# A sliding-window attention and gated-MLP kernel whose work is ordered by a list scheduler, with 64-key half-blocks in tiled arrays

## The chip, the core and the metric

The kernel runs on one core of a Trainium2 chip. The metric is the device time of one execution in microseconds; the kernel before took 304.65 us (median of 3 runs, 304.59 to 305.05). The engines are PE (TensorE, matrix products from SBUF into PSUM), PEld (its weight loads), DVE (VectorE), ACT (ScalarE), POOL (GpSimd) and SP (SyncE, which here only issues transfers). PSUM has eight banks of 128 partitions x 512 fp32 numbers. Each engine works through its own instruction stream in order.

## The reference

```python
def reference(A_x, A_wqkv, A_wo, B_x, B_w_gate, B_w_up, B_w_down):
    def _A_ref(x, wqkv, wo):
        B, S, D = x.shape
        H = 32; Dh = D // H; W = 256
        ...
        scores = jnp.einsum("bhqd,bhkd->bhqk", q, k) * (Dh ** -0.5)
        idx = jnp.arange(S)
        mask = (idx[:, None] - idx[None, :] >= 0) & (idx[:, None] - idx[None, :] < W)
        scores = jnp.where(mask[None, None], scores, -1e9)
        p = _softmax(scores, axis=-1)
        ...
    def _B_ref(x, w_gate, w_up, w_down):
        ...
        h = g * u
        ...
    x = A_x
    xn = _layernorm(x, axis=-1)
    return x + _A_ref(xn, A_wqkv, A_wo) + _B_ref(xn, B_w_gate, B_w_up, B_w_down)
```

There are 2048 tokens of width 512, 32 heads of 16 numbers, an inner width of 1792, all in bf16. A query sees itself and the 255 tokens before it. Attention and the gated product both read the normalised input, and both are added to x.

## The kernel before

Tokens go in four chunks T of 512, each of four blocks b of 128. All weights are loaded once and stay in SBUF (`setup`): the first blocks of x, then gate and up weights, the rest of x, down and output weights on SP's queue, Wqkv in three parts on ACT's queue (values first, then keys, then queries).

**Normalising.** `norm_stats` (L114, L115, DVE), `norm_scale` (L123, L125, POOL), `norm_apply` (L133, DVE) make xn. `norm_transpose` turns a block by four PE transposes (L145) into PSUM and copies it to xnT, on ACT for the first chunk (L148), on DVE later (L150).

**Projections.** `proj_v` (L157) gives values, which ACT copies (L159). `proj_qk` (L167) gives keys or queries for eight heads; DVE copies them and makes a second key tile Ko, in which the even heads are zeroed (L170, L171, L174). In the first chunk `proj_qk_block` (L183) does this block by block for the first eight heads alone, and their other 24 heads come later as fillers.

**Attention.** For a chunk, eight heads c, and even or odd heads par, there are three steps i. `scores` (L201) multiplies key blocks of 128 by the query blocks that see them, by the table GROUPS: a tuple is (key block, first and last query block, column). Four heads run side by side as row tiles of 32 partitions and write the four banks of S, the only score buffer. ACT takes the exponential of all four banks at once into P (L209, 2048 elements per partition), and POOL zeroes the triangles at the window's two edges by `affine_select` (L214, L218), 128 columns of four heads at a time. `values` (L234) multiplies the strips of three steps by V, four heads side by side as column tiles, and accumulates in one bank, `accb`. A column of ones in V gives the sums. DVE transposes the result in blocks of 32 (L245), divides (L247, L248) and transposes back to OT (L251).

**Gated product.** `gate` (L261), copied by DVE to gsb (L264), `up` (L270), multiplied by gsb into hT (L272), then `down` (L279) over hT, with the output projection `wo` (L284) added in the same bank; `store` adds x (L291) and sends the block out (L292). In the last chunk `finish_early` adds three quarters of the output projection and x (L303), and `finish_late` the last quarter. All dense results share three banks (`ps_m`).

**Order.** `run` does the first chunk's norm and projections block by block, then goes through 96 score steps. Between them it places dense work from the list `fillers` in proportion to the steps' weight, and `values` two steps after the last scores of a group. On the other engines the order is that in which the work was written.

## Time and profile before

| what | before |
|---|---|
| median of 3 runs | 304.65 us (304.59 to 305.05) |
| profiled execution: span from first to last instruction | 299.1 us |
| what lies around the span (median less span) | 5.55 us |
| PE busy | 274.7 us |
| DVE busy | 194.3 us |
| ACT busy | 181.5 us |
| POOL busy | 156.8 us |
| ACT's exponentials (L209) | 96, 170.0 us |
| POOL's selects (L214, L218) | 240, 154.6 us |

The profile lists one execution. A group is a source line with its engine, its tiles and shape; "x4" counts instructions, and the bracket at the end of a timeline row is the idle time of the engine just before it and what ended it. Matmuls are pipelined: the duration of one contains its way through the array, so durations in a row overlap, and the distance between starts says what one costs.

### The profile page before, as it was taken

How to read it: one execution, taken by the hardware profiler on the slowest of the kernel's cores; microseconds unless marked ns; L12 is line 12 of the kernel's file. 1: busy time of each engine (PE TensorE's matmuls, PEld its weight loads, DVE VectorE, ACT ScalarE, POOL GpSimd, SP SyncE). 2: the span in 40 equal slices, each digit the busy share in tenths (PEclk: the TensorE clock that was granted, in tenths of full speed). 3: DMA queues.
4: the chain of work that ended last, by engine and by line, in shares of the span. 5: the costliest groups of instructions: out<-in, count | busy, mean ns of one | idle time of the engine just before them, and what ended most of it. 6: DMA issues, size and time to landing. Idle time of an engine off the chain costs nothing.

```text
span 299.1 us, 5877 instructions
## 1 busy us (share of the span) xinstructions
PE 274.7 (92%) x2424; PEld 119.6 (40%) x2460; DVE 194.3 (65%) x362; ACT 181.5 (61%) x118; POOL 156.8 (52%) x266
## 2 busy tenths in 40 slices
PE   6569989999999999999999999999999999999992
PEld 5333333433433444444344444443444443344440
DVE  3238898985823599984942489985763357877325
ACT  1247566568766756669566666758766675756610
POOL 3115565455565556656555466655556555555620
PEclk9999999999999999999999999999999999999998
DMA  7999000000000100000000000000000000000001
GB/s 234 370 369 324 3 3 0 3 0 2 1 20 18 37 0 2 1 2 2 0 19 19 20 18 3 0 2 1 2 0 20 35 20 1 2 0 2 2 0 70
DMA packets 10506, 12.17 MB, mean 41 GB/s; under 512 B 496, under 2 KB 10480, under 8 KB 10480
## 3 DMA queue, kind: packets, MB, share of 16 engines
q1 hardware_dynamic: 8896, 10.23, 10.1%
q10 hardware_dynamic: 1584, 1.57, 1.7%
q8 instruction: 19, 0.31, 0.4%
q14 instruction: 7, 0.06, 0.1%
HBM read 9.70 MB, written 2.10 MB: 39 GB/s over the span
## 4 chain that ended last, share of the span: by engine, by line
PE 68%; ACT 17%; DVE 6%; DMA 3%; issue 3%; POOL 1%; ACTq 1%; DVEq 0%
ACT P L209 16%; PE psd L279 15%; PE up L270 12%; PE gp L261 11%; PE S L201 10%; PE accb L234 7%; PE qkp L167 6%; DMA Wqkv<-in_A_wqkv_dram 3%; PE vp L157 2%; PE psd L284 2%; DVE at L245 1%; PE xTp L145 1%; DVE hT L272 1%; DVE st L114 1%; PE qkb L183 1%
## 5 line engine op out<-in xcount | busy, mean ns | idle before, releaser
L209 ACT ACTIVATE P<-S 128x2048 bf16<-128x2048 f32 (+2 forms) x96 | 170.0, 1771 | 86.8 <-PE S L201 79.1
L214 POOL TENSOR_SCALAR_AFFINE_SELECT P<-P 128x512 bf16<-128x512 bf16 x128 | 81.8, 639 | 75.2 <-ACT P L209 74.6
L218 POOL TENSOR_SCALAR_AFFINE_SELECT P<-P 128x512 bf16<-128x512 bf16 x112 | 72.8, 650 | 42.4 <-ACT P L209 42.4
L261 PE MATMUL gp<-xnT,Wg 128*128 128x512 bf16 x213 | 57.1, 380 | 1.4 <-DVE gsb L264 0.5
L270 PE MATMUL up<-xnT,Wu 128*128 128x512 bf16 x216 | 57.3, 380 | 0.5
L279 PE MATMUL psd<-Wd,hT 128*128 128x512 bf16 x213 | 51.7, 380 | 1.4 <-issue 1.3
L272 DVE TENSOR_TENSOR hT<-up,gsb 128x512 bf16<-128x512 f32 x56 | 38.5, 687 | 11.0 <-PE up L270 8.0
L245 DVE STREAM_TRANSPOSE at<-accb 128x512 f32<-128x512 f32 x32 | 22.9, 715 | 32.6 <-PE accb L234 32.2
L264 DVE CAST gsb<-gp 128x512 bf16<-128x512 f32 x56 | 38.1, 680 | 3.7 <-PE gp L261 3.4
L270 PEld LDWEIGHTS <-Wu 128*128 128x128 bf16 x224 | 19.9, 98 | 25.8 <-issue 5.4
L279 PEld LDWEIGHTS <-hT 128*128 128x128 bf16 x224 | 19.8, 97 | 25.9 <-issue 5.3
L261 PEld LDWEIGHTS <-Wg 128*128 128x128 bf16 x224 | 19.8, 98 | 25.0 <-issue 6.0
L167 PE MATMUL qkp<-xnT,Wqkv 128*128 128x512 bf16 x117 | 27.5, 380 | 0.5 <-issue 0.5
L234 PE MATMUL accb<-P,V 128*17 128x384 bf16 (+2 forms) x704 | 25.4, 276 | 0.0
L291 DVE TENSOR_TENSOR y<-psd,x 128x512 bf16<-128x512 f32 x12 | 8.3, 692 | 23.2 <-PE psd L284 23.2
L201 PE MATMUL S<-Q,Ko 32*128 32x256 bf16 (+2 forms) x352 | 18.4, 275 | 3.8 <-ACT P L209 3.6
L201 PE MATMUL S<-Q,K 16*128 16x256 bf16 (+2 forms) x352 | 18.4, 275 | 2.6 <-ACT P L209 2.4
L234 PEld LDWEIGHTS <-V 128*17 128x17 bf16 x704 | 13.8, 90 | 8.7 <-issue 5.5
L167 PEld LDWEIGHTS <-Wqkv 128*128 128x128 bf16 x120 | 10.7, 98 | 13.7 <-issue 2.5
L157 PE MATMUL vp<-Wqkv,xnT 128*128 128x512 bf16 x61 | 15.9, 392 | 0.3 <-issue 0.2
L201 PEld LDWEIGHTS <-Ko 32*128 32x128 bf16 x352 | 6.9, 92 | 22.6 <-issue 22.1
L201 PEld LDWEIGHTS <-K 16*128 16x128 bf16 x352 | 6.6, 92 | 22.6 <-issue 22.5
(44 smaller groups left out, 172.2 us busy)
## 6 DMA issues: line engine op xcount, KB each, us to landing
out_dram<-y SPq DMA_DIRECT2D x16, 128.0 KB, 1.7
Wg<-in_B_w_gate_dram SPq DMA_DIRECT2D x2, 896.0 KB, 9.9
Wu<-in_B_w_up_dram SPq DMA_DIRECT2D x2, 896.0 KB, 11.5
Wd<-in_B_w_down_dram SPq DMA_DIRECT2D x1, 1792.0 KB, 17.7
Wqkv<-in_A_wqkv_dram ACTq DMA_DIRECT2D x3, 512.0 KB, 6.0
x<-in_A_x_dram SPq DMA_DIRECT2D x1, 1024.0 KB, 14.6
x<-in_A_x_dram SPq DMA_DIRECT2D x4, 128.0 KB, 5.1
x<-in_A_x_dram SPq DMA_DIRECT2D x1, 512.0 KB, 8.2
```

Of the source, the lines that this page charges most:

```text
L167: nc.tensor.matmul(ps[:], lhsT=self.Wqkv[:, k, lo:lo + 128], rhs=self.xnT[T][:, k, :], start=(k == 0), stop=(k == 3))
L201: nc.tensor.matmul(S[:, e, col:col + n], lhsT=(self.Ko if par else self.K)[U][rows, c, 128 * j:128 * j + 128], rhs=self.Q[T][rows, c, 128 ...
L209: nc.scalar.activation(out=P[:, :, lo:hi], in_=S[:, :, lo:hi], func=ACT.Exp, scale=0.25)
L214: nc.gpsimd.affine_select(out=P[:, :, j:j + 128], in_=P[:, :, j:j + 128], pattern=[[0, 4], [1, 128]], compare_op=ALU.is_ge, fill=0.0, base ...
L218: nc.gpsimd.affine_select(out=P[:, :, j:j + 128], in_=P[:, :, j:j + 128], pattern=[[0, 4], [-1, 128]], compare_op=ALU.is_gt, fill=0.0, bas ...
L234: nc.tensor.matmul(acc[32 * e:32 * e + 17, 128 * q0:128 * q0 + n], lhsT=self.V[U][:, v, 8 * c + 2 * e + par, 0:17], rhs=P[:, e, col:col + ...
L245: nc.vector.transpose(out=at.rearrange("p b r -> p (b r)"), in_=acc[:])
L261: nc.tensor.matmul(ps[:], lhsT=self.Wg[:, k, 128 * f:128 * f + 128], rhs=self.xnT[T][:, k, :], start=(k == 0), stop=(k == 3))
L264: nc.vector.tensor_copy(out=self.gsb[:], in_=ps[:])
L270: nc.tensor.matmul(ps[:], lhsT=self.Wu[:, k, 128 * f:128 * f + 128], rhs=self.xnT[T][:, k, :], start=(k == 0), stop=(k == 3))
L272: nc.vector.tensor_tensor(out=self.hT[T][:, f, :], in0=ps[:], in1=self.gsb[:], op=ALU.mult)
L279: nc.tensor.matmul(self.psd[:], lhsT=self.hT[T][:, f, 128 * b:128 * b + 128], rhs=self.Wd[:, f, :], start=(f == 0), stop=False)
```

## The change

The whole program is written anew around a list scheduler that runs while the program is built. Each piece of work on DVE, ACT, POOL and SP is an `Op` with what it depends on and, for each engine that could do it, a duration from a table in the file; PE's work is a list of `Dense` pieces, of `Sums` (the down and output projections), score batches and value steps. `loop` always takes the piece that can start first by these figures and writes it to the engine's stream. The order that results is fixed; on the chip the engines wait for one another by semaphores as before.

- **Half-blocks.** A key block has 64 keys, and `layout` says which query blocks of 64 it meets: (key block, first query block, how many, column). A score matmul holds the 64 keys of an even and an odd head in one stationary tile of 32 rows x 128 columns; keys are stored twice, each with the other head's rows zeroed (`i_keys`, written straight from PSUM by ACT or DVE). There are 76 score batches instead of 96, five for a chunk and eight heads (four in the first chunk).
- **Value steps.** One step takes both heads: eight tiles of 64 rows x 32 columns, into two banks. There are 16 value steps with 96 matmuls each (72 in the first chunk) instead of 32 with 24 (16). There is no bank of its own for them: four banks are shared by dense results and values.
- **V in column halves.** `add_v` projects 64 tokens for even and 64 for odd heads side by side, 16 matmuls of 256 columns for a block instead of four of 512.
- **Masks.** A batch with four masked blocks gets two ANDs on DVE with mask tiles (56 in all, 512 elements per partition); the others get POOL selects on 64 partitions (240 of 256 elements and 8 of 512).
- **Transposes.** The first chunk is turned by PE as before, the other three by 12 transposing DMAs on SP's queue.
- **First chunk.** Keys and queries of all 32 heads are projected block by block, 128 matmuls of 128 columns. Scores begin after that. The root of the variance is taken by ACT and DVE instead of POOL, with one more table load on ACT. Wqkv is loaded in parts on both queues between the blocks of x.
- **Copies** from PSUM go to DVE or ACT as the scheduler finds; 15 of the 56 gate copies go to ACT. P has seven buffers instead of five.
- **End.** The last value step is followed by 83 dense matmuls; the last block is summed in two column parts (320 and 192) and stored by two queues.

```diff
-GROUPS = (
-    ((-2, 0, 0, 0), (0, 0, 2, 128)),
-    ((-1, 0, 1, 0), (2, 2, 3, 256)),
-    ((1, 1, 3, 0), (3, 3, 3, 384)),
-)
+MM = 0.2158
+SWITCH = 0.11
+PE_LAT = {"V": 0.22, "A": 0.31}
+LAT = 0.06
+KEYS_COPY = {"V": (0.68, 0.76), "A": (0.63, 0.70)}
+PSUM_COPY = {"V": (0.605, 0.69), "A": (0.49, 0.60)}
...
+def layout(T):
+
+
+    if T == 0:
+        return [[(2, 2, 4, 0), (4, 4, 4, 4)], [(0, 0, 5, 0), (5, 5, 3, 5)],
+                [(1, 1, 5, 0), (6, 6, 2, 5), (7, 7, 1, 7)], [(3, 3, 5, 0), (2, 6, 1, 5)]]
+    return [[(3, 3, 5, 0), (-3, 0, 2, 5), (-4, 0, 1, 7)], [(2, 2, 5, 0), (6, 6, 2, 5), (7, 7, 1, 7)],
+            [(0, 0, 5, 0), (5, 5, 3, 5)], [(1, 1, 5, 0), (-2, 0, 3, 5)], [(-1, 0, 4, 0), (4, 4, 4, 4)]]
...
+def masked(batch):
+
+
+    return sorted((at + i, (q + i - k) // 4) for k, q, m, at in batch for i in range(m) if q + i - k in (0, 4))
...
+    PBUFS = 7
+    WINDOW = 4
+    PACE = 2.9
+    SHARE = 1.0
+    FEED = 0.1
+    HOLD = 0.2
+    TURN = 0.2
...
+        self.S = psum.tile([128, 4, 512], F32, name="S")
+        self.M = [psum.tile([128, 512], F32, name=f"M{i}") for i in range(4)] + [self.S[:, 3, :]]
...
+        load(nc.sync, self.x[0:64, 0, :], xv[0:64, 0, :])
+        load(nc.scalar, self.x[64:128, 0, :], xv[64:128, 0, :])
+        load(nc.sync, self.x[:, 1, :], xv[:, 1, :])
+        qkv(nc.sync, 1024, 0, 2)
+        qkv(nc.scalar, 1024, 2, 4)
+        qkv(nc.scalar, 512, 2, 4)
+        qkv(nc.sync, 512, 0, 2)
+        load(nc.sync, self.x[:, 2, :], xv[:, 2, :])
+        qkv(nc.sync, 0, 0, 4)
+        load(nc.sync, self.x[:, 3, :], xv[:, 3, :])
...
+    def i_scores(self, T, c, batch):
+
+        for k, q, m, at in batch:
+            U, j = divmod(8 * T + k, 8)
+            for e in range(4):
+                rows = slice(32 * e, 32 * e + 32)
+                self.nc.tensor.matmul(
+                    self.S[:, e, 64 * at:64 * (at + m)],
+                    lhsT=self.K[U % 3][rows, c, j].rearrange("p l t -> p (l t)"),
+                    rhs=self.Q[T % 2][rows, c, 64 * q:64 * (q + m)],
+                    start=True, stop=True, tile_position=(32 * e, 0), skip_group_check=True)
...
+    def i_select(self, P, lane, kind, at, n):
+        v = P[64 * lane:64 * lane + 64].rearrange("p e (b q) -> p e b q", q=64)[:, :, at:at + 4 * n - 3:4, :]
+        sign = -1 if kind else 1
+        self.nc.gpsimd.affine_select(out=v, in_=v, pattern=[[0, 4], [0, n], [sign, 64]], base=0, fill=0.0,
+                                     compare_op=ALU.is_gt if kind else ALU.is_ge, channel_multiplier=-sign)
+
+    def i_and(self, P, at, step, n, row):
+        v = P.bitcast(I16).rearrange("p e (b q) -> p e b q", q=64)[:, :, at:at + (n - 1) * step + 1:step, :]
+        m = self.masks[:, row:row + n, :].unsqueeze(1).to_broadcast([128, 4, n, 64])
+        self.nc.vector.tensor_tensor(out=v, in0=v, in1=m, op=ALU.bitwise_and)
...
+    def i_values(self, T, c, strips, banks):
+        rest = sorted(((P, s) for P, batch in strips for s in batch), key=lambda x: x[1][2])
...
+        for n, (P, (k, q, m, at)) in enumerate(segments):
+            U, j = divmod(8 * T + k, 8)
+            for lane in range(2):
+                rows = slice(64 * lane, 64 * lane + 64)
+                for e in range(4):
+                    self.nc.tensor.matmul(
+                        banks[lane][32 * e:32 * e + 17, 64 * q:64 * (q + m)],
+                        lhsT=self.V[U % 3][rows, j, 4 * c + e, 0:17],
+                        rhs=P[rows, e, 64 * at:64 * (at + m)],
+                        start=n == 0, stop=n == len(segments) - 1, tile_position=(64 * lane, 32 * e),
+                        skip_group_check=True)
...
+    def i_keys(self, e, T, c, lane, in_, blocks=slice(0, 8)):
+
+        own = self.own[:, lane:lane + 1]
+        out = self.K[T % 3][:, c, blocks, lane, :]
+        in_ = in_.rearrange("p c (j t) -> p c j t", t=64)
+        if e == "A":
+            self.nc.scalar.activation(out=out, in_=in_, func=ACT.Copy, scale=own)
+        else:
+            self.nc.vector.tensor_scalar(out=out, in0=in_, scalar1=own, scalar2=None, op0=ALU.mult)
...
+    def loop(self):
+        while True:
+            best, now0 = None, self.first_s is None
+            for o in self.waiting:
+                t = self.when(o.deps)
+                if t is None:
+                    continue
+                for e, (took, lat) in o.on.items():
+                    at = max(t, self.free[e])
+                    key = (at + (0.3 if e == "A" and len(o.on) > 1 and not now0 else 0.0) + (self.HOLD if o.rank and now0 else 0.0), o.rank, t)
+                    if best is None or key < best[0]:
+                        best = (key, o, e, at)
...
+            if best is None:
+                break
+            _, o, e, at = best
+            took, lat = o.on[e]
+            o.start, o.eng, o.end = at, e, at + lat + LAT
+            self.free[e] = at + took
+            self.waiting.remove(o)
+            self.log.append((at, e, took, o.name))
+            if self.live:
+                o.emit(e)
...
+    def do_scores(self, at):
+        g = self.g
...
+        hi = 64 * max(s[3] + s[2] for s in batch)
+        took = 0.000833 * 4 * hi
+        ex = self.op(f"exp{g}", {"A": (took + 0.06, took + 0.18)}, [o], lambda e: self.nc.scalar.activation(
+            out=P[:, :, 0:hi], in_=self.S[:, :, 0:hi], func=ACT.Exp, scale=0.25), rank=0)
+        self.at_["S", g] = ex
+        last = ex
+        if len(masked(batch)) > 3:
+            for m in ands(batch):
+                cost = 4 * 64 * m[2] * 0.00055 + 0.07
+                last = self.op(f"and{g}", {"V": (cost, cost + 0.08)}, [ex, last, ("masks",)], lambda e, m=m: self.i_and(P, *m), rank=1)
...
+    def do_values(self, at):
+        v, banks = self.v, [self.take_bank(), self.take_bank()]
+        self.v += 1
+        T, c = self.pairs[v]
...
+        ts = []
+        for par in range(2):
+            t = self.op(f"tr{v}", {"V": (0.63, 0.71)}, [o] + ts, lambda e, par=par: nc.vector.transpose(
+                out=self.at[:, :, par, :], in_=self.M[banks[par]].rearrange("p (b r) -> p b r", r=32)), rank=1)
+            self.frees(t, banks[par])
...
+            def project(i, lo, tok=tok):
+                for k in range(4):
+                    for c in range(4):
+                        self.nc.tensor.matmul(
+                            self.M[i][:, 128 * c:128 * c + 128], lhsT=self.Wqkv[:, k, lo + 128 * c:lo + 128 * c + 128],
+                            rhs=self.xnT[0][:, k, tok], start=k + c == 0, stop=k == 3, skip_group_check=True)
...
+    def norms(self, T):
+        w = T % 2
+        begin = [("gate", T - 1, 0)]
+        st = [self.op(f"st{T}.{b}", {"V": (0.96, 1.05)}, begin, lambda e, b=b: self.i_stats(4 * T + b, self.mv[w]),
+                      rank=8) for b in range(4)]
+        r = self.op(f"rs{T}", {"G": (1.05, 1.1)}, st, lambda e: self.i_root(w, 4 * T, 4), rank=0)
+        for b in range(4):
+            ap = self.op(f"ap{T}.{b}", {"V": (0.38, 0.48)}, [r], lambda e, b=b: self.i_apply(4 * T + b), rank=7)
+            deps = [ap] + ([("up", T - 2, NF - 1)] if T > 1 else [])
+            self.at_["xnT", T, b] = self.op(f"dt{T}.{b}", {"S": (1.5, 3.0)}, deps, lambda e, b=b: (
+                self.nc.sync.dma_start_transpose(out=self.xnT[w][:, :, 128 * b:128 * b + 128], in_=self.xn[b][:])),
+                rank=1)
+
...
+    def add_v(self, T, b, land=0.0):
+
+        def emit(i):
+            for k in range(4):
+                for jj in range(2):
+                    tok = slice(128 * b + 64 * jj, 128 * b + 64 * jj + 64)
+                    w = self.Wqkv[:, k, 1024:1536].rearrange("p (h l d) -> p l h d", l=2, d=16)
+                    for lane in range(2):
+                        self.nc.tensor.matmul(self.M[i][64 * lane:64 * lane + 64, 256 * jj:256 * jj + 256],
+                                              lhsT=self.xnT[T % 2][:, k, tok], rhs=w[:, lane], start=k + jj == 0,
+                                              stop=k + jj == 4, tile_position=(0, 64 * lane), skip_group_check=True)
```

**PE around a boundary inside a value step.** Before, in a value step of a later chunk (accb is its one bank, P the strips, V1 and V2 the values of two chunks), a stretch of four matmuls passes to the next key block:

```order
L234 LDWEIGHTS V1_913
L234 MATMUL accb_116<-P_2340,V1_913 17x128
L234 LDWEIGHTS V2_1872
L234 MATMUL accb_116<-P_2340,V2_1872 17x384
L234 LDWEIGHTS V2_1872
```

In the new program, inside a value step, the same weights' block passes from the even heads' bank M0 to the odd heads' bank M2:

```order
L253 MATMUL M0_111<-P3_90,V1_79 17x256
L253 LDWEIGHTS V1_79
L253 MATMUL M0_111<-P3_90,V1_79 17x256
L253 LDWEIGHTS V1_79
L253 MATMUL M2_113<-P3_90,V1_79 17x256
```

Four tiles with one bank became eight tiles with two, and the matmuls of a stretch are those of one 64-key block.

**ACT around the third chunk's projections.** Before, it copies V alone (vp is the bank of values, S the scores):

```order
L209 ACTIVATE P<-S 128x4x256
L209 ACTIVATE P<-S 128x2048 x22
L159 ACTIVATE V_1872<-vp 128x32x16 x2
L209 ACTIVATE P<-S 128x2048
L159 ACTIVATE V_1872<-vp 128x32x16 x2
L209 ACTIVATE P<-S 128x2048 x23
```

In the new program it takes copies of all kinds between exponentials (M are the four shared banks, gsb the gate's copy):

```order
L290 ACTIVATE K_77<-M_112,own 128x8x64
L506 ACTIVATE P_92<-S 128x2048
L209 ACTIVATE V_80<-M_113 128x32x16
L506 ACTIVATE P_93<-S 128x2048
L506 ACTIVATE P_87<-S 128x2048
L209 ACTIVATE Q_73<-M_114 128x512
L506 ACTIVATE P_88<-S 128x2048
L209 ACTIVATE Q_73<-M_113 128x512
L506 ACTIVATE P_89<-S 128x2048
```

One copy at most stands between two exponentials there; K, Q and gsb came over from DVE.

**SP.** Before, the loads are followed by the stores alone:

```order
L68 DMA Wu<-in_B_w_up_dram 128x4x896
L69 DMA x<-in_A_x_dram 128x8x512
L70 DMA Wd<-in_B_w_down_dram 128x14x512
L71 DMA Wo<-in_A_wo_dram 128x4x512
L292 DMA out_dram<-y 128x512 x16
```

In the new program the transposing DMAs of the three later chunks stand between loads and stores:

```order
L685 DMA_TRANSPOSE xnT0_81<-xn3_97 128x4x128
L800 DMA out_0_dram<-y_1505 128x512
L800 DMA out_0_dram<-y_1664 128x512
L800 DMA out_0_dram<-y_1704 128x512
L800 DMA out_0_dram<-y_1868 128x512
L685 DMA_TRANSPOSE xnT1_82<-xn0_94 128x4x128
L800 DMA out_0_dram<-y_2548 128x512
L685 DMA_TRANSPOSE xnT1_82<-xn1_95 128x4x128
```

Each transposing DMA waits for its normalised block, and what follows on SP waits behind it.

850 lines of the change are left out of this document (511 added, 339 removed).

## The prediction

> **What bounds the kernel now.** I read the busy row first, then TensorE's order of time in one steady stretch, then the waits, and last the two ends of the span.
>
> ```profile
> span 299.1 us, 5877 instructions
> PE 274.7 (92%) x2424; PEld 119.6 (40%) x2460; DVE 194.3 (65%) x362; ACT 181.5 (61%) x118; POOL 156.8 (52%) x266
> PEclk9999999999999999999999999999999999999998
> PE 68%; ACT 17%; DVE 6%; DMA 3%; issue 3%; POOL 1%; ACTq 1%; DVEq 0%
> ```
>
> TensorE is busy for 92% at full clock, and it holds 68% of the chain that ended last. No other engine passes 65%. But matmuls overlap, so what each stretch really costs is the distance from its start to the next start, on the steady timeline of PE (start, duration, instruction, idle before it):
>
> ```profile
> 116.88 1.03 PE L270 MATMUL up<-xnT,Wu 128*128 128x512 bf16 x4
> 117.84 0.40 PE L201 MATMUL S<-Q,K 16*128 16x384 bf16 x8
> 118.22 1.02 PE L261 MATMUL gp<-xnT,Wg 128*128 128x512 bf16 x4
> 119.08 1.03 PE L270 MATMUL up<-xnT,Wu 128*128 128x512 bf16 x4
> 120.30 0.40 PE L201 MATMUL S<-Q,Ko 32*128 32x128 bf16 x8 [0.19 <-ACT P L209]
> 120.63 1.04 PE L261 MATMUL gp<-xnT,Wg 128*128 128x512 bf16 x4
> 121.50 1.03 PE L270 MATMUL up<-xnT,Wu 128*128 128x512 bf16 x4
> 122.37 0.39 PE L145 MATMUL xTp<-ident,xn 128*128 128x128 bf16 x4
> 122.75 0.40 PE L201 MATMUL S<-Q,Ko 32*128 32x256 bf16 x8
> 123.08 0.83 PE L234 MATMUL accb<-P,V 128*17 128x128 bf16 x24
> 123.85 0.39 PE L261 MATMUL gp<-xnT,Wg 128*128 128x512 bf16 x1
> ```
>
> The price of one dense matmul of 512 columns comes from an unbroken run in the chain of waits:
>
> ```profile
> 283.95 3.02 PE psd L279 x14
> ```
>
> That is 3.02/14 = 0.216 us, so a column costs 0.216/512 = 0.42 ns. In the steady rows four dense matmuls take 0.87 us, and 0.96 us ahead of scores (116.88 to 117.84): entering the tiled mode costs 0.10. A score step of 512 columns takes 0.33 us (120.30 to 120.63); 0.21 is columns, 0.12 leaving. So a score step between dense work costs 0.43. The 24 value matmuls (four side by side, 1536 columns, 0.64 us) take 0.77, again 0.13 over the columns. Four transposes take 0.38 in this place.
>
> The only repeated wait on PE is that of scores for the exponential that empties S, their one buffer (total, times, longest):
>
> ```profile
> ACT P L209 <- PE S L201: 79.1, 82, 1.9
> PE S L201 <- ACT P L209: 6.1, 23, 0.6
> ```
>
> This view counts from the modelled end of a matmul. At 120.30 it shows 0.19, while the starts lie 1.22 apart instead of 0.96, so 0.26 is lost. With 0.07 more for each of 23, I take 8 us. The cycle behind it:
>
> ```profile
> 118.37 1.88 ACT L209 ACTIVATE P<-S 128x2048 bf16<-128x2048 f32 x1 [1.92 <-PE S L201]
> ```
>
> From the start of the scores (117.84) to the exponential 0.53, then 1.88, then 0.05 to the next scores: 2.46 us between two score steps at least.
>
> **The change part by part.** *Dense work* stays: gate, up, down and output projection and the later q and k are the same 832 matmuls' worth of 512 columns; nothing is gained. The first chunk's q and k become 128 matmuls of 128 columns; the row for eight of those is below (0.44 us, 0.055 each), so 7.0 us against 24 x 0.216 + 32 x 0.055 = 6.9. Zero.
>
> *Attention columns.* Before: 80 score steps at 0.43 and 16 shorter ones of the first chunk (384 or 256 columns, so 0.38 or 0.33), 40.0 us; 24 value steps at 0.77 and 8 of the first chunk:
>
> ```profile
> 30.07 0.67 PE L234 MATMUL accb<-P,V 128*17 128x384 bf16 x16
> 30.67 0.39 PE L270 MATMUL up<-xnT,Wu 128*128 128x512 bf16 x1
> ```
>
> at 0.60, 23.3 us. Together 63.3. With 64-key blocks a query block meets five half-blocks (320 keys) instead of three blocks (384): 2560 columns for a head group instead of 3072, and 76 score steps instead of 96. The 16 value steps run eight tiles at once, 2560 columns or 1920. By columns: 72 x 0.43 + 4 x 0.38 = 32.5; 12 x (1.07 + 0.13) + 4 x (0.80 + 0.12) = 18.1; together 50.6, a gain of 12.7.
>
> But a stretch of 64 columns lasts 27 ns, and weights for it must be loaded meanwhile. What a weight load takes, and how loads and matmuls begin in the first 0.03 us of a value step (two windows of the same step):
>
> ```profile
> L234 PEld LDWEIGHTS <-V x704: 87/92/92, 30.1 to 290.2; 128*17 128x17 bf16 x176
> 114.38 0.23 PE L234 MATMUL accb<-P,V 128*17 128x128 bf16 x4
> 114.37 0.11 PEld L234 LDWEIGHTS <-V 128*17 128x17 bf16 x8 [0.21 <-issue]
> ```
>
> In the window to 114.39 four matmuls have started, and by 114.40 eight loads: tiles start together, but only one set is loaded ahead. So I let no stretch pass in under 0.09 us. Of the 12 stretches of a value step (5, 2, 1, 5, 2, 1, 5, 3, 5, 3, 4, 4 blocks) six are shorter: +0.22 each step, +0.17 in the first chunk, +0.04 for each of 28 score batches with three stretches; 4.4 us. **Term: -8.3** (from -12.7 to +11, the upper end in the rivals).
>
> *Transposes on PE*: 48 of 64 go to DMAs. Twelve times four, between 4 x 0.055 = 0.22 and 0.38: **-3.2** (-2.6 to -4.6). Their copies from PSUM leave DVE. The transposing DMA has no row here; the nearest is a plain one of the same 128 KB:
>
> ```profile
> out_dram<-y SPq DMA_DIRECT2D x16, 128.0 KB, 1.7
> ```
>
> In the new order some 35 us of PE work lie between the first gate matmul and the first use of the next chunk's transposed input. Statistics and scaling take 9 to 14 of it, so about 25 are left for four transposes: hidden at 1.7 us each, late from 6 us each. They stand on SP ahead of output stores, and only those queue behind them.
>
> *Score waits.* In the new order of PE, pricing what lies between two score steps with the rows above gives 2.59 us (ten dense matmuls) at the least and mostly 3.02 (twelve), all over 2.46. ACT's 76 exponentials fit, and a copy of 0.6 fits the 0.53 in which scores are computed. Late here and there: 1.5 us stay. **Term: -6.5** (-8 to 0).
>
> *The start.* PE before the first scores:
>
> ```profile
> 10.37 0.61 PE L183 MATMUL qkb<-xnT,Wqkv 128*128 128x128 bf16 x4 [1.65 <-DMA Wqkv<-in_A_wqkv_dram]
> 13.97 0.61 PE L183 MATMUL qkb<-xnT,Wqkv 128*128 128x128 bf16 x8 [0.69 <-ACT xnT L148]
> 14.41 1.03 PE L157 MATMUL vp<-Wqkv,xnT 128*128 128x512 bf16 x4
> 16.27 0.40 PE L145 MATMUL xTp<-ident,xn 128*128 128x128 bf16 x4 [0.84 <-DVE xn L133]
> 17.36 0.61 PE L183 MATMUL qkb<-xnT,Wqkv 128*128 128x128 bf16 x8 [0.68 <-ACT xnT L148]
> 21.40 0.34 PE L201 MATMUL S<-Q,K 16*128 16x384 bf16 x4
> ```
>
> From 10.37 to 21.40, 11.0 us, the work is 28 x 0.055 + 16 x 0.216 + 12 x 0.055 = 5.7; 5.3 are waits for the norm chain. Now PE holds 2.6 us of q, k, v work per block (32 x 0.055 + 4 x 0.216) while the next is normalised, and it need not wait for the last third of Wqkv before the values. First scores come when all four blocks are projected, about 17 us, but with 5.2 us of what used to follow already done and eight gate matmuls. **Term: -7** (0 to -9).
>
> *Values of V in column halves*: 256 matmuls of 256 columns in pairs, the same columns, 8 more mode changes: **+1**. If their 256 weight loads, about 0.09 like those above, stood one by one, a pair would take 0.18 for 0.11: +9.
>
> *Masks.* POOL's 240 selects become 248 at half width:
>
> ```profile
> L214 POOL TENSOR_SCALAR_AFFINE_SELECT P<-P 128x512 bf16<-128x512 bf16 x128 | 81.8, 639 | 75.2 <-ACT P L209 74.6
> L78 POOL TENSOR_SCALAR_AFFINE_SELECT ident<-ident 128x128 bf16<-128x128 bf16 x1 | 0.3, 292 | 0.1
> ```
>
> Between 0.29 and 0.64, so 0.41 for 256: some 102 us, hidden. DVE gains 56 ANDs and two masked copies for K, loses 15 gate copies to ACT and the separate Ko:
>
> ```profile
> L264 DVE CAST gsb<-gp 128x512 bf16<-128x512 f32 x56 | 38.1, 680 | 3.7 <-PE gp L261 3.4
> L171 DVE TENSOR_SCALAR Ko<-K,odd x15: 353/354/825, 23.5 to 218.9; 128x512 bf16<-128x512 bf16 x15
> ```
>
> An AND costs 0.35 to 0.83 (the row's least and most; I take 0.53): +30. Thirteen V copies and seven more for K at 0.68: +14; 15 gate and 9 Q copies to ACT -16, Ko -8, transposed copies -5. DVE rises to about 210 us of a shorter span: over 75%, still behind PE. But dense results and value results now share four banks, and a value step keeps two until DVE has transposed them: **+1.5** (0 to +12).
>
> *The end.*
>
> ```profile
> 292.87 0.95 PE L284 MATMUL last<-Wo,OT 128*128 128x512 bf16 x3 [0.70 <-DVE OT L251]
> 294.04 0.38 PE L284 MATMUL last<-Wo,OT 128*128 128x512 bf16 x1 [0.22 <-DVE y L291]
> 295.83 0.69 DVE L291 TENSOR_TENSOR y<-last,y 128x512 bf16<-128x512 f32 x1 [0.66 <-DMA out_dram<-y]
> ```
>
> PE waits 0.92, the last add waits 0.66 for a buffer and handles 512 columns; now 83 matmuls cover the last transposes, and the last tile goes out in two parts: **-2.5** (0 to -3).
>
> Sum: -8.3 - 3.2 - 6.5 - 7 + 1 + 1.5 - 2.5 = -25.0. The profiled execution has a span of 299.1; the median is 304.65, so 5.55 lie outside the span and stay. 304.65 - 25.0 = 279.65: **280 us**. Its own range: 272 if weight loads and banks cost nothing; 288 if the start gains nothing.
>
> **The rivals.** *A: value matmuls pass one by one.* 24 matmuls in 0.64 us is 27 ns each, so the average of the old kernel can't exclude it. 96 x 0.027 = 2.56 instead of 1.29 in twelve steps, 72 x 0.027 = 1.92 instead of 0.97 in four: +19, **299 us**. The four that started within 0.01 us speak against it. By the Trainium skill, "TensorE: Matmul & The Clock Gate", "Wait — 56ns, not 53.3ns?", matmuls never start under about 25 ns apart however few columns they have; by that estimate the time would be about 297. The four starts in 0.01 us disagree with it for tiles. Chance 0.07.
>
> *B: DVE holds the banks.* If each of 16 value steps finds one more operation of 0.6 us ahead of its transposes, PE stands 16 x 0.6 = 10 us: **290 us**. For: DVE over 75%, ANDs up to 0.83. Against: the copies moved to ACT. Chance 0.13.
>
> *C: slower, by the transposing DMAs.* If a transpose takes t, the second chunk's first projections wait 4t - 25 us on PE. The gain of 25 is gone at t = 12.5; at 14 it is 31, **311 us**. For: no row shows one. Against: 1.7 us for the plain store, seven times less. Chance 0.05. The Trainium skill, "VectorE: DVE Perf Modes", "The three transpose paths", gives 1309 ns for a 128x128 crossbar transpose; four for an instruction and four instructions would be an estimated 21 us, inside the 25. No run so far shows one.
>
> *D: the new order doesn't hold on the chip*, since its queues are fixed and waits return elsewhere: start, score waits and end gain nothing, and banks cost 10.5: -8.3 - 3.2 + 1 + 10.5 = 0, **304.65 us**, no change. Chance 0.02.
>
> **How the numbers follow.** The forecast has 0.73. A measurement can tell about 0.2% (0.6 us). Faster holds the forecast, A and B: 0.93; same 0.02 (D); slower 0.05 (C). The range, 270 to 295, runs from the lower bounds of start and banks through B; A, C and D lie outside, 0.14, and the forecast's own tails.
>
> **What would show it.** Right: score steps between dense work still at about 0.43, value steps 1.3 to 1.5 us, hardly a wait of scores for the exponential, first scores near 17 us, transposes landing in a few us. Wrong: value steps over 2 us (A); dense matmuls that wait for DVE (B); a gap ahead of the second chunk's projections (C); exponentials further apart than 3 us (D).

## The result, and the profile after

| | before | after |
|---|---|---|
| median | 304.73 us (304.59 to 305.05) | 266.35 us (266.16 to 267.99) |
| profiled execution: span | 299.1 us | 264.0 us (266.31 with what lies around it) |

The ratio is 0.878 (95% interval 0.872 to 0.884): 38.4 us less. The forecast was 280 us, and its range ended at 270. The direction and most of the mechanisms were right; the gain was half as large again as forecast, and which terms were too small is the subject of what follows.

The page of the new kernel, with its busy row, the granted clock and the chain that ended last:

```profile
span 264.0 us, 7965 instructions
...
PE 256.2 (97%) x3420; PEld 131.7 (50%) x3456; DVE 189.2 (72%) x366; ACT 166.4 (63%) x124; POOL 119.3 (45%) x272
...
PEclk9999999999999999999999999999999999999999
...
PE 93%; DMA 2%; issue 2%; ACT 1%; DVE 1%; SPq 0%; DVEq 0%; ACTq 0%
```

TensorE went from 92% to 97% busy and from 68% to 93% of the chain; ACT's 17% of the chain fell to 1%. All waits of PE by the view of waits (total, times, longest):

```profile
PE M L215 <- issue: 1.7, 11, 0.2
PE M L205 <- PEq L827: 0.8, 1, 0.8
PE M L632 <- DVE xn L281: 0.6, 1, 0.6
```

The row of scores waiting for the exponential (6.1 us, 23 times) has no successor, and no dense matmul waits for DVE to empty a bank. The 1.7 us of "issue" stand where the record of a first dense matmul is missing. The steady timeline of PE, in the same place as the forecast's:

```profile
125.04 1.90 PE L215 MATMUL M<-xnT,Wqkv 128*128 128x512 bf16 x8
126.77 1.03 PE L215 MATMUL M<-xnT,Wg 128*128 128x512 bf16 x4
127.73 0.40 PE L223 MATMUL S<-Q,K 32*128 32x320 bf16 x12
128.06 1.29 PE L253 MATMUL M<-P,V 64*17 64x256 bf16 x96
129.28 1.04 PE L215 MATMUL M<-xnT,Wu 128*128 128x512 bf16 x3
```

Start to start: eight dense matmuls 1.73 (0.216 each, as before), four ahead of scores 0.96, scores 0.33, and the whole value step 1.22 (1.22 and 1.23 where no record is missing). A value step of the first chunk takes 0.94:

```profile
32.99 1.01 PE L253 MATMUL M<-P,V 64*17 64x256 bf16 x72
33.93 1.04 PE L215 MATMUL M<-xnT,Wg 128*128 128x512 bf16 x3
```

The start of PE, and its end with DVE's last add and the last store:

```profile
8.12 2.84 PE L647 MATMUL M<-xnT,Wqkv 128*128 128x128 bf16 x48
10.80 0.39 PE L632 MATMUL M<-ident,xn 128*128 128x128 bf16 x4
11.03 1.95 PE L647 MATMUL M<-xnT,Wqkv 128*128 128x128 bf16 x32
...
17.54 0.40 PE L223 MATMUL S<-Q,K 32*128 32x256 bf16 x8
```

```profile
257.56 3.08 PE L215 MATMUL M<-Wo,OT 128*128 128x512 bf16 x15
...
260.48 0.49 PE L215 MATMUL S<-Wo,OT 128*128 128x192 bf16 x4
261.14 0.35 DVE L793 TENSOR_TENSOR xn<-S,x 128x192 bf16<-128x192 f32 x1
261.52 0.37 ACTq L800 DMA_DIRECT2D out_dram<-xn  x1
```

First scores come at 17.54 instead of 21.40, with the q and k of every head already projected, but the V of one block only instead of four. After the last matmul's end (260.97) 3.0 us are left; before it was 294.42 and 4.7. Last, the groups of masks on the two engines, from the page, and the transposing DMAs from the view of DMA issues (count, median us to landing):

```profile
L232 POOL TENSOR_SCALAR_AFFINE_SELECT P<-P 64x256 bf16<-64x256 bf16 (+1 forms) x248 | 112.3, 455 | 106.6 <-ACT P L506 94.3
...
L238 DVE TENSOR_TENSOR P<-P,masks 128x512 int16<-128x512 int16 x56 | 22.3, 406 | 8.6 <-ACT P L506 8.6
```

```profile
xnT<-xn SPq DMA_TRANSPOSE x12, 3.5
```

### The profile page after: what moved, and what is told of

Same layout as the page of the kernel before. It is cut to its first block, busy times and chain, and to the rows that moved or that the text cites. A ratio compares the mean times of both kernels' runs of the same rounds, so it can differ in the third digit from the quotient of the medians.

```text
span 264.0 us, 7965 instructions
## 1 busy us (share of the span) xinstructions
PE 256.2 (97%) x3420; PEld 131.7 (50%) x3456; DVE 189.2 (72%) x366; ACT 166.4 (63%) x124; POOL 119.3 (45%) x272
## 4 chain that ended last, share of the span: by engine, by line
PE 93%; DMA 2%; issue 2%; ACT 1%; DVE 1%; SPq 0%; DVEq 0%; ACTq 0%
PE M L215 68%; PE S L223 10%; PE M L253 7%; PE M L699 6%; PE M L647 3%; DMA x<-in_A_x_dram 1%; ACT P L506 1%; DMA out_dram<-xn 1%; PE M L632 1%; PE S L215 0%; DVE xn L793 0%; SPq L151 0%; DVE st L599 0%; DVEq L838 0%; DVE xn L281 0%
## 5 line engine op out<-in xcount | busy, mean ns | idle before, releaser
L506 ACT ACTIVATE P<-S 128x2048 bf16<-128x2048 f32 x76 | 140.9, 1853 | 56.2 <-PE S L223 47.7
L232 POOL TENSOR_SCALAR_AFFINE_SELECT P<-P 64x256 bf16<-64x256 bf16 (+1 forms) x248 | 112.3, 455 | 106.6 <-ACT P L506 94.3
L215 PE MATMUL M<-xnT,Wg 128*128 128x512 bf16 x219 | 57.4, 380 | 0.3
L215 PE MATMUL M<-xnT,Wu 128*128 128x512 bf16 x213 | 56.6, 380 | 0.4
L215 PE MATMUL M<-Wd,hT 128*128 128x512 bf16 (+1 forms) x214 | 50.6, 374 | 1.4 <-issue 1.3
L751 DVE TENSOR_TENSOR hT<-M,gsb 128x512 bf16<-128x512 f32 x56 | 38.3, 684 | 6.9 <-PE M L215 6.6
L211 DVE CAST gsb<-M 128x512 bf16<-128x512 f32 x41 | 28.1, 686 | 6.4 <-PE M L215 6.1
L223 PE MATMUL S<-Q,K 32*128 32x320 bf16 (+3 forms) x720 | 30.1, 254 | 0.4
L542 DVE STREAM_TRANSPOSE at<-M 128x512 f32<-128x512 f32 x32 | 21.4, 699 | 11.7 <-PE M L253 11.7
L238 DVE TENSOR_TENSOR P<-P,masks 128x512 int16<-128x512 int16 x56 | 22.3, 406 | 8.6 <-ACT P L506 8.6
L215 PE MATMUL M<-xnT,Wqkv 128*128 128x512 bf16 x90 | 22.6, 380 | 0.3
L699 PEld LDWEIGHTS <-xnT 128*64 128x64 bf16 x256 | 13.4, 110 | 1.9 <-issue 1.6
```

The costliest lines, as they stand in the source:

```text
L211: self.nc.vector.tensor_copy(out=out, in_=in_)
L215: self.nc.tensor.matmul(ps, lhsT=a, rhs=b, start=first and n == 0, stop=last and n == len(pairs) - 1)
L223: self.nc.tensor.matmul(self.S[:, e, 64 * at:64 * (at + m)], lhsT=self.K[U % 3][rows, c, j].rearrange("p l t -> p (l t)"), rhs=self.Q[T % ...
L232: self.nc.gpsimd.affine_select(out=v, in_=v, pattern=[[0, 4], [0, n], [sign, 64]], base=0, fill=0.0, compare_op=ALU.is_gt if kind else ALU ...
L238: self.nc.vector.tensor_tensor(out=v, in0=v, in1=m, op=ALU.bitwise_and)
L506: ex = self.op(f"exp{g}", {"A": (took + 0.06, took + 0.18)}, [o], lambda e: self.nc.scalar.activation(out=P[:, :, 0:hi], in_=self.S[:, :, ...
```

## The experiments

Unless a text says otherwise, a kernel computes the reference and is compared with the 266.35 us of the new kernel.

### What a value step costs

**Stretches in ascending length.** The new kernel mixes long and short stretches (one stretch is the eight matmuls of one key block); here the short ones come first, one after another.

```diff
-        keep, segments, t = rest.pop(0), [], 0.0
-        while rest:
...
-        segments.append(keep)
+        segments = rest
```

> The new kernel with the stretches of a value step in ascending length (1, 1, 2, 2, 3, 3 blocks first, then 4 and 5) instead of long and short ones mixed. Theory 1: weights for a stretch of eight tiles take about 0.09 us to load, and the mixed order hides that by letting loads run ahead under long stretches; then six short stretches in a row show it, the value step of 96 matmuls goes from 1.22 to about 1.45 us, and the time rises by 12 x 0.23 + 4 x 0.17, 3 to 4 us, to about 270. Theory 2: there is no such floor, the 4.4 us of the forecast were wrong as a mechanism; then the step stays at 1.22 and the time at 266.3.

Measured: 267.87 us (267.24 to 269.64). The step of the steady part in its PE timeline:

```profile
130.86 1.37 PE L248 MATMUL M<-P,V 64*17 64x64 bf16 x96
132.17 1.04 PE L215 MATMUL M<-xnT,Wu 128*128 128x512 bf16 x3
```

1.31 instead of 1.22, and 1.00 instead of 0.94 in the first chunk: together 1.2 of the 1.5 us. The four short stretches stand first: two of one block, 0.027 us each by their columns, and two of two blocks, 0.053 each. Three windows on the same step, up to 130.98, 131.08 and 131.09, show how many matmuls have started; eight are one stretch:

```profile
130.86 0.30 PE L248 MATMUL M<-P,V 64*17 64x64 bf16 x24
130.86 0.36 PE L248 MATMUL M<-P,V 64*17 64x64 bf16 x32
130.86 0.46 PE L248 MATMUL M<-P,V 64*17 64x64 bf16 x33
```

Start to start, the four take 0.035, 0.029, 0.056 and 0.103 us, and each of the others 0.002 to 0.003 over its columns. Only the fourth is late, by 0.05, and 0.03 more pass between the last stretch and the dense work. So a stretch has no least time of 0.09: one of 64 columns passes in 0.028 to 0.035, although each of its eight weight loads lasts 0.083 to 0.088, since these loads overlap (the first 32 start within 0.12 us). What holds up the fourth is open. In the mixed order nothing does.

**The two heads' halves in turn.** The same 96 matmuls, but all of the even heads' four tiles first, then all of the odd heads' four, so that, but for the turn between the two, only four tiles are at work.

```diff
-        for n, (P, (k, q, m, at)) in enumerate(segments):
-            U, j = divmod(8 * T + k, 8)
-            for lane in range(2):
-                rows = slice(64 * lane, 64 * lane + 64)
+        for lane in range(2):
+            rows = slice(64 * lane, 64 * lane + 64)
+            for n, (P, (k, q, m, at)) in enumerate(segments):
+                U, j = divmod(8 * T + k, 8)
```

> The new kernel with the value steps' matmuls in another order: all stretches of the even heads (four tiles of the upper 64 rows), then all of the odd heads (lower 64 rows), instead of both in each stretch. Same instructions, same banks. Theory 1: eight tiles run side by side only if they are issued together; then a step of 96 takes 2 x 1.07 + 0.16 = 2.3 instead of 1.23 us, and the time rises by 12 x 1.07 + 4 x 0.80 = 16 us, to about 283. Theory 2: what a step costs is the passing of its matmuls one by one, at some 12 ns each, and not its columns; then the order is of no account, and the time stays at 266 to 268.

Measured: 279.73 us (278.89 to 280.49), 13.4 more.

```profile
134.62 2.14 PE L253 MATMUL M<-P,V 64*17 64x256 bf16 x96
136.69 1.04 PE L215 MATMUL M<-xnT,Wu 128*128 128x512 bf16 x4
```

2.07 instead of 1.22. (By columns alone two halves are 2 x 1.07 = 2.13; they overlap a little at the turn.) Eight tiles really work side by side in the new kernel, and that by itself is worth 13 us. This also settles rival A from the other side.

### What the waits of scores cost

**Scores close together in the new kernel.** The planner believes that an exponential takes 1.02 us plus a little instead of 1.71, and is allowed a score step each 2.2 us, so it puts less dense work between two of them.

```diff
-    PACE = 2.9
+    PACE = 2.2
...
-        took = 0.000833 * 4 * hi
+        took = 0.0005 * 4 * hi
```

> The new kernel with the planner's figures for the exponential (0.0005 us per element instead of 0.000833) and for the pace of score steps (2.2 us instead of 2.9) made too low, nothing else; the instructions are the same ones in another order. By the rows of before the work between two score steps is now 2.16 us in most places, 0.3 under the 2.46 that a cycle of scores and exponential takes, 17 us short in all. Theory 1: the spacing is what removed the waits of scores; then they come back, 15 to 17 us in all, about 282. Theory 2: PE has other reasons to be free of waits (seven strip buffers, copies shared with ACT), and the spacing hardly matters; then under 5 us, 266 to 271.

Measured: 282.06 us (281.81 to 283.67), 15.7 more. The wait of the kernel before is back as the largest of PE:

```profile
PE S L223 <- ACT P L506: 10.4, 44, 0.4
```

Same instructions, another spacing: the spacing removes the waits. As in the kernel before, the view shows less than the time lost. Summed from start to start, the last dense matmuls ahead of scores take 23.7 us more than their columns, against 7.5 in the new kernel's second run: about 16, so the loss lies there.

**Half an exponential in the kernel before.** The kernel before, kept busy at its start (below), with exponential and masks on two of the four banks of scores; the values read those two twice. So half of the exponential is left out, and PE's instructions are unchanged.

```diff
-        nc.scalar.activation(out=P[:, :, lo:hi], in_=S[:, :, lo:hi], func=ACT.Exp, scale=0.25)
+        nc.scalar.activation(out=P[:, 0:2, lo:hi], in_=S[:, 0:2, lo:hi], func=ACT.Exp, scale=0.25)
...
-                                     rhs=P[:, e, col:col + n], start=first, stop=(i == 2),
+                                     rhs=P[:, e % 2, col:col + n], start=first, stop=(i == 2),
```

> The kernel before, kept busy at its start as in the earlier run, but the exponential and the masks handle only two of the four banks of scores, and the value matmuls read those two twice: half of the exponential is left out, so an exponential takes about 1 us instead of 1.88 and no score step has to wait for the one before it. TensorE's instructions are the same. Theory 1 (the waits of scores for the exponential cost the kernel before about 10 us, which is what a sum of the starts leaves over): 301.6 - 10 = about 291.5 us, with 1 us less if the first chunk's start gains too. Theory 2 (they cost 8, as forecast): 293.6. Theory 3 (they cost the 6.1 us of the view of waits): 295.5.

Measured: 294.35 us (293.98 to 294.66) against 301.63: 7.3 us less (measured on another chip, on which the kernel before had 301.78 instead of 302.87). Its exponential takes 1.02 (ACT's timeline), and scores wait for none of them:

```profile
118.75 1.02 ACT L215 ACTIVATE P<-S 128x1024 bf16<-128x1024 f32 x1 [1.46 <-PE S L207]
```

That lies between the second theory (8) and the third (6.1), nearer the second; the first, 10 us left over from a sum of starts, falls. The traces say where the difference is. From start to start, the 91 dense matmuls ahead of scores take 16.8 us more than their columns in the kernel kept busy and 8.7 with half an exponential, which is what entering the tiled mode costs. So the waits themselves were 8.1, as forecast; 0.8 of it came back as longer score steps (0.5) and waits for DVE (0.3).

### The start

**The kernel before once more**, unchanged, for the granted clock of its first 30 us.

> The kernel before, unchanged, once more with a profile. The forecast let 5.55 us lie around the span (304.65 less 299.1) and stay; the new kernel has 266.31 less 264.0, so 2.3. Theory 1: about 2.3 us lie around the span of either kernel, and the first profile of before was an execution some 3 us shorter than the timed ones; then time less span of the same execution is 2.3 here too. Theory 2: the old kernel really has 5.5 us around its span (something at its start or end that isn't an instruction), and the change took 3.2 us of it away; then time less span is about 5.5 here.

Measured: 304.41 us (301.31 to 305.25). The profiled execution took 304.18 with a span of 302.5, so 1.7 us lie around it, not 5.55. By windows (PE busy first, clock behind the engines):

```profile
5.00:7.50 2.50, 0.55 (x7) 0.32 (x5) 1.18 (x3) 0.35 (x1) 1.13 (x3) 1.00 1.10 360
7.50:10.00 2.50, 0.38 (x4) 0.21 (x3) 0.00 (x0) 0.25 (x1) 0.00 (x0) 0.62 1.11 352
10.00:15.00 5.00, 3.82 (x20) 2.26 (x22) 1.65 (x6) 1.19 (x2) 0.86 (x2) 0.50 1.06 379
15.00:20.00 5.00, 4.32 (x20) 2.03 (x19) 2.30 (x8) 1.19 (x2) 0.86 (x2) 0.50 1.06 379
20.00:25.00 5.00, 3.90 (x22) 2.08 (x22) 0.75 (x3) 1.56 (x3) 0.00 (x0) 0.50 1.10 349
```

The pauses, and the first scores, in PE's timeline:

```profile
6.71 0.40 PE L145 MATMUL xTp<-ident,xn 128*128 128x128 bf16 x4 [1.56 <-DVE xn L133]
7.80 0.38 PE L183 MATMUL qkb<-xnT,Wqkv 128*128 128x128 bf16 x4 [0.69 <-ACT xnT L148]
10.28 0.61 PE L183 MATMUL qkb<-xnT,Wqkv 128*128 128x128 bf16 x4 [2.10 <-DMA Wqkv<-in_A_wqkv_dram]
...
24.42 0.51 PE L201 MATMUL S<-Q,K 16*128 16x384 bf16 x4 [0.36 <-issue]
```

The row from 7.5 to 10 (0.62) puts the fall to half clock at 8.1 us. The pauses of 1.56 and 0.69 lie before it; the one of 2.10 begins only then. Half clock lasts to 25 us, and the first scores come at 24.42 instead of the 21.40 of the earlier profile. That profile's clock row reads 1.00 from the start, but the starts of its matmuls say otherwise:

```profile
10.37 0.61 PE L183 MATMUL qkb<-xnT,Wqkv 128*128 128x128 bf16 x4 [1.65 <-DMA Wqkv<-in_A_wqkv_dram]
10.77 0.63 PE L157 MATMUL vp<-Wqkv,xnT 128*128 128x512 bf16 x1
```

Four matmuls of 128 columns take 0.40 us, 0.10 each, where eight take 0.44 from 13.97 on. So PE ran at half speed there up to some 13 us, and at full speed from then on; in the second profile it was fast from 4.7 on, lost that at 8.1 and got it back at 25. The first execution was among the shortest (later spans are 299.2 to 303.5), and the median is not: 299.1 + 1.7 = 300.8 against 304.7.

**The kernel before, kept busy.** Matmuls of 128 columns whose result nothing reads fill the pauses of the start.

```diff
-        for _ in range(36):
+        for _ in range(48):
...
+            if b == 0 and j == 1:
+                self.busy(30)
...
+            self.busy(8)
             self.proj_qk_block(b)
             self.proj_v(b)
+            self.busy(12)
```

> The kernel before with idle-time matmuls added at its start, into the bank accb that nothing reads yet: 12 more at the warm-up, 30 while the query weights are on their way, and 20 around each block of the first chunk (0.055 us each, in places where PE waited 0.7 to 2 us). No other work changes. Theory 1: the old kernel's pauses of 0.7 to 2.1 us before 25 us make PE's clock fall to half in many executions (0.50 between 10 and 25 us in its second profile, first scores at 24.42 instead of 21.40), and its median holds about 3 us of that; with the pauses filled the clock stays at 1.0, the first scores come at about 21.4 in every execution, and the times gather at 301 to 302 instead of 301 to 305. Theory 2: the clock falls for another reason (the loads' traffic), and the added work only delays the chain; then the spread stays and the median is the same or 1 to 3 us higher.

Measured: 301.63 us (301.37 to 302.14, 12 runs) against 302.87 of the kernel before on the same chip (301.03 to 304.88); the ratio is 0.995 (0.992 to 0.998).

```profile
7.50:10.00 2.50, 2.26 (x40) 2.14 (x40) 0.00 (x0) 0.60 (x1) 0.58 (x1) 1.00 1.10 349
10.00:15.00 5.00, 4.18 (x52) 3.03 (x50) 1.78 (x7) 1.19 (x2) 0.86 (x2) 1.00 1.06 377
```

Useless work makes the kernel faster and its runs alike. Of the 17 executions of the kernel before, the ten with a mean granted clock of 0.973 or less took 302.8 to 304.9 us, and the seven with 0.979 or more 301.0 to 301.9; kept busy, all twelve had 0.993 or more. DMA traffic is the same (the last two columns), so the fall follows from PE's pauses and costs 2 to 3 us in the executions that it meets. The added matmuls themselves cost something: first scores come at 22.66, not at the expected 21.4. The new kernel fills most of the same pauses with q and k.

**First chunk by heads in the new kernel**, instead of all heads block by block; then the same with the planner's pace at 3.0 instead of 2.9.

```diff
...
-            self.add(f"k0b{b}", 4.4, [("xnT", 0, b), wk], lambda i, f=project: f(i, 512), k_out)
-            self.add(f"q0b{b}", 4.4, [("xnT", 0, b), wq], lambda i, f=project: f(i, 0), q_out)
+        for c in range(4):
+            self.add_qk(0, c)
```

> The new kernel, but keys and queries of the first chunk are projected as in the later chunks (eight heads at a time, 512 columns, after all four blocks are turned) instead of block by block for all heads. The columns are the same. Theory 1: the 7 us of key and query work per block are what fills PE while the norm chain runs; without them PE waits in the first chunk, only 3.5 us of value work being left to fill some 7 us, so 4 to 6 us more, 270 to 273, and perhaps a lower clock there. Theory 2: the earlier loads and the shorter norm chain give the gain at the start; then scores even begin earlier and the time stays within 2 us of the new kernel's.

> The first chunk projected by heads as in the run before (279.66 us), but planned with a pace of 3.0 us for score steps instead of 2.9, so that no two score steps lie over 3.5 us apart and 83 dense matmuls again follow the last value step. In the earlier run PE's start was only some 2.6 us of work behind at 17.5 us, and at the end scores and the last value step stood with nothing between them, with waits of 2.0, 2.5, 0.5 and 0.8 us and the clock at half. Theory 1: the start by heads costs only these 2 to 3 us, and the other 10 were the uneven end of that plan; then 268 to 270. Theory 2: the start by heads itself costs 13 us (waits and clock further on); then about 279 again.

Measured: 279.66 us (279.17 to 280.56), and with the other pace 270.03 us (269.15 to 270.64). The end of the first one's PE timeline shows why they differ:

```profile
252.64 0.40 PE L223 MATMUL S<-Q,K 32*128 32x320 bf16 x8
255.06 0.40 PE L223 MATMUL S<-Q,K 32*128 32x256 bf16 x8 [2.03 <-ACT P L506]
258.00 0.34 PE L253 MATMUL M<-P,V 64*17 64x256 bf16 x4 [2.54 <-POOL P L232]
258.86 3.14 PE L253 MATMUL M<-P,V 64*17 64x256 bf16 x92 [0.52 <-POOL P L232]
262.81 7.80 PE L215 MATMUL M<-Wd,hT 128*128 128x512 bf16 x28 [0.81 <-DVE at L542]
```

The plan had used its dense work too early, and the last scores and values stand with nothing between them: 5.9 us of waits, and a value step at a lowered clock (0.50 from 258.1 to 268.3). With an even plan, the first chunk by blocks is worth 270.03 - 266.35 = 3.7 us. The traces agree: at its first scores (17.21) this kernel has done 6.2 us of projections by their prices, the new one at 17.54 has done 9.7: 3.5 more in 0.3 us. Edits to a planned kernel move the plan's end too; only the second run tests the start.

### Banks, sharing of copies and masks, transposes

**Three shared banks instead of four**, first at the same pace, then at 3.0.

```diff
...
-        self.banks = [0.0] * 4
+        self.banks = [0.0] * 3
...
```

> The new kernel with three shared banks instead of four until the last dense sums begin (the fourth is cleared at the start and joins then). Theory 1: the banks are what keeps PE free of waits, since a value step holds two until DVE has transposed them; with one bank left PE waits some 0.8 us at each of 16 value steps, 13 us, about 279. Theory 2: copies out of PSUM keep up with three as well, the forecast's 1.5 us for banks were a price for nothing; then only the few score steps that the planner now puts closer than 2.46 us cost something, 2 us, about 268.

> Three shared banks as in the run before (278.79 us), planned with a pace of 3.0 us, so that the plan ends like the new kernel's (27 matmuls, the last value step, 83 matmuls). In the earlier run PE's idle in the steady part was only 2 to 3 us above the new kernel's, and the end had waits of 2.6 and 0.8 us, a fall of the clock and hardly any dense work between the last scores. Theory 1: three banks make PE wait at each value step, 0.8 us x 16, whatever the plan; then about 278. Theory 2: three banks cost 2 to 5 us, and the rest was the end of the plan; then 268 to 272.

Measured: 278.79 us (278.34 to 280.24), with the same uneven end as above, and 271.75 us (270.7 to 272.07) with an even plan. So the fourth bank is worth 4 to 5 us (270.7 against 266.16 by the shortest executions). In the profile 2.1 lie before the first scores (at 19.69 instead of 17.54), but only half of that is the banks': a pause of 0.58 for a copy. The rest is a later rise to full speed, as the first 16 matmuls of V take 1.85 us from start to start instead of 1.05. That differs from execution to execution: it is 1.85 also in the profile of the kernel with close scores, which has four banks, and 1.00 in that of three banks at the first pace. With four banks the view shows no wait for one.

**All copies from PSUM on DVE.**

```diff
-KEYS_COPY = {"V": (0.68, 0.76), "A": (0.63, 0.70)}
-PSUM_COPY = {"V": (0.605, 0.69), "A": (0.49, 0.60)}
+KEYS_COPY = {"V": (0.68, 0.76)}
+PSUM_COPY = {"V": (0.605, 0.69)}
```

> The new kernel without copies out of PSUM on ACT after the first transposes (gate, V, K and Q copies can only go to DVE); planned anew, and the plan has no gap over 4 us and ends with 94 dense matmuls. DVE's load rises from 189 by about 34 x 0.69 = 23 to 212 us, 80%. Theory 1: DVE behind PE at 80% holds banks longer, 0.3 us at each of some 16 value steps, 4 to 8 us, 270 to 274. Theory 2: the planner spreads the copies well enough that PE never waits; then 266 to 268, and the sharing with ACT is worth nothing.

Measured: 267.92 us (267.8 to 269.34): 1.6 more, though DVE is at 78%:

```profile
PE 260.3 (97%) x3456; PEld 132.3 (49%) x3456; DVE 208.9 (78%) x403; ACT 146.7 (55%) x87; POOL 120.7 (45%) x272
```

That is the DVE time that the forecast feared for rival B (about 210 us), and PE still does not wait for it in the steady part. Nearly all of the 1.6 lies before the first scores, in pauses of 0.52, 0.23 and 0.69 for copies, which the new kernel's profile does not have.

**All masks on POOL.**

```diff
-        if len(masked(batch)) > 3:
+        if len(masked(batch)) > 9:
```

> The new kernel with all masks on POOL (no ANDs on DVE): 216 more selects of 256 elements at 0.455 us, so POOL's 119 us become about 215 of 266, and a full group needs 32 x 0.455 = 14.6 us of some 15.5 us. DVE loses 22 us. The plan has no gap over 4 us and ends as before. Theory 1: POOL becomes nearly as loaded as PE, strips come late to the value steps and PE waits there, more as the delay adds up over a chunk; 270 to 285. Theory 2: seven strip buffers take up the delay, POOL still follows; 266 to 268, and the ANDs are worth nothing.

Measured: 274.6 us (273.44 to 275.67), 8.2 more. POOL's group grows to 472 selects:

```profile
L232 POOL TENSOR_SCALAR_AFFINE_SELECT P<-P 64x256 bf16<-64x256 bf16 (+1 forms) x472 | 209.0, 456 | 23.1 <-ACT P L506 4.6
```

```profile
PE M L253 <- POOL P L232: 4.2, 10, 0.7
```

From start to start, the 16 value steps take 26.07 us in all, against 18.44 in the new kernel's second run: 7.6 of the 8.2 are waits inside them. So POOL at 79%, the only engine to mask the strips between scores and values, makes values wait, and the 56 ANDs on DVE are worth 8 us.

**Transposes of the later chunks on TensorE again**, at the pace of 3.0.

```diff
-            self.at_["xnT", T, b] = self.op(f"dt{T}.{b}", {"S": (1.5, 3.0)}, deps, lambda e, b=b: (
-                self.nc.sync.dma_start_transpose(out=self.xnT[w][:, :, 128 * b:128 * b + 128], in_=self.xn[b][:])),
...
+            for k in range(4):
+                self.nc.tensor.transpose(self.psT(i)[:, k, :], self.xn[b][:, 128 * k:128 * k + 128], self.ident[:])
```

> The new kernel, but the transposes of the later chunks' normalised input are made by TensorE again, as in the kernel before (12 times four of 128 columns, with 12 copies out of PSUM by ScalarE or VectorE), instead of by 12 transposing DMAs; the planner's pace is 3.0 instead of 2.9, so that the plan still ends with dense work under its last stretches. Theory 1 (moving the transposes off TensorE is worth what the forecast priced, 4 x 0.055 = 0.22 to 0.38 each): 12 x 0.22 to 0.38 is 2.6 to 4.6 us, so 266.4 + 3.2 = 269.6 us (269.0 to 271.0). Theory 2 (the gain of 38 owes more to this than was priced, because transposes in the middle of the steady work also take a bank and a place in VectorE's or ScalarE's queue): 273 us or more. Theory 3 (the pace alone costs as much as the transposes): about 267 with the transposes nearly free.

Measured: 269.24 us (268.81 to 269.41), 2.9 more, as the first theory has it: 12 x 0.24. From start to start its twelve transposes take 2.9 us in all, so the pace of 3.0 costs nothing beside them. In the kernel before the twelve take 3.9, 0.7 of it a wait for DVE behind the second.

**The new kernel again**, for its spread.

> The new kernel, unchanged, as the measure for the three others on the same chip: 266 to 268 us, granted clock 1.0 through the start, since its PE has no pause of over 1 us after the first 6 us.

Measured: 266.37 us (266.31 to 266.62).

## Why the prediction was wrong

The forecast's steps are worked against the profiled span of before, so they answer to 299.1 - 264.0 = 35.1 us. The column "measured" sums, from start to start, what PE's traces hold for each step. Inside the steady part it uses the kernel before kept busy and the new kernel's second run, since in these no matmul record is missing; from the first scores to the last matmul's start they take 272.6 and 243.2 us, as the two first profiles do.

| step | forecast | measured | from |
|---|---|---|---|
| attention columns | -8.3 | -12.0 | scores, values and entering the tiled mode: 63.1 to 51.0 |
| score waits | -6.5 | -8.1 | ahead of scores 16.8 over the columns, 8.7 with half an exponential |
| the start | -7 | -8.2 | 3.9 earlier, with 4.3 of later work done (5.2 of q and k and 1.7 of gate and up, less 2.6 of V) |
| transposes | -3.2 | -3.9 | 2.8, and 1.0 of waits for DVE around one of them |
| V in column halves | +1 | +0.8 | mode changes around them |
| banks | +1.5 | -0.4 | no wait for DVE; before, one of 0.4 at a gate matmul |
| the end | -2.5 | -3.2 | 1.4 between the last matmuls, and 5.1 to 3.3 from the last one's start on |
| remainder | | -0.1 | |
| span | -25.0 | -35.1 | |
| clock at the start, by medians | 0 | -3.9 | 299.1 + 1.7 against 304.7 |
| time around the span | 0 | +0.6 | 1.7 to 2.3 |

Three steps failed.

- **"So I let no stretch pass in under 0.09 us."** Here 4.4 us were given back of a gain by columns of 12.7, of which 12.0 came. The forecast took the length of one weight load as the least time of a stretch, reading that only one set is loaded ahead. The loads of a stretch last 0.083 to 0.088 each, but overlap: stretches of 64 columns pass in 0.028 in the mixed order, and a whole step in 1.22, 1.07 of columns and the mode change. Even the ascending order shows no such floor. The cautious value was taken although the forecast had itself quoted four tiles that start within 0.01 us.
- **"So 5.55 lie outside the span and stay."** A median of some executions was set against the span of another. Around the span lie 1.7 us in the kernel before; the other 3.9 were half clock at the start, which the profiled execution had for a shorter time (to 13 us) than the second one (to 25), and which the change mostly removes by filling PE's pauses. A second profile showed it, and the first had a hint: its matmuls of 128 columns at 10.37 stand 0.10 apart. So of the 5.3 us that the forecast took for waits of the norm chain 1.3 were half speed, and "at full clock" does not hold for the first 13 us. The size of the term is in part the luck of the draw of four executions: later medians of the kernel before are 301.8 to 302.9 (7 to 17 executions each) and 304.4 (eight), so up to 2 to 3 us of it can be chance.
- **"Banks: +1.5", and the 1.5 us of score waits that were to stay.** Both were allowances for an order that does not quite hold on the chip. It holds: no wait is left. With DVE at 209 us there is still none in the steady part, and even with three banks the loss was 4 to 5 us, so the bound of 12 was too high as well.

Smaller misses with the same sign are the transposes and the end (0.7 each), where PE had waited for DVE longer than the forecast had seen, and the start (1.2). The forecast's items for the start, 4.4 us earlier with 5.2 and 1.7 of later work done, add up to 11.3, not 7; the V of three blocks, which now follows the first scores, takes 2.6 back.

Some sums of the forecast do not come out as written. "272 if weight loads and banks cost nothing" is 279.65 - 4.4 - 1.5 = 273.8, and 272.3 only if no score wait stays either; without a gain at the start it is 286.7, not 288. The range's end of 270 needs the lower bounds of the stretches and score waits beside those of start and banks, which alone give 276.2. At 25 ns for each value matmul the time comes to 296, not 297. The measured 266.35 lies below every one of these lower ends.

What held: the price of a dense matmul, of a score step (0.33 and 0.10) and of the pairs of V's halves, and the 8 us for the waits of scores. DVE has 189 us, not 210: an AND takes 0.41, not 0.53 (7 us), and the reciprocals and products of the value steps, 16 larger ones instead of 32, take 5 less, which the forecast left out; the rest is spread over small groups.

Rival A (one by one) is excluded: 96 matmuls in 1.22 us are 13 ns each, where 27 were its price. By the Trainium skill, "TensorE: Matmul & The Clock Gate", "Wait — 56ns, not 53.3ns?", starts lie at least about 25 ns apart; this trace disagrees for eight tiles side by side. Within one stretch their starts lie about 3 ns apart. Rival B did not happen, and C did not either: the transposing DMAs landed in 3.5 us (2.4 to 7.3), and none of PE's waits is for them.

## What to carry to other kernels

Price work on TensorE from start to start in the trace, and where a price is unknown on one side only, let the likeliest value follow the nearest row instead of a safe one: three such allowances (3.7 for the stretches, 1.5 for banks, 1.6 for waits) cost this forecast nearly 7 us. Compare a span with a time only of the same execution, and look at the clock of more than one profile, by its row and by the distance of equal matmuls, before the difference between them is called fixed. In a kernel whose order is planned, an edit moves the plan's end: see whether dense work is left there before a slower time is blamed on the edit.
